# Five VectorE instructions per decoded weight tile in place of seven, with a second ScalarE pass and an integer addition

## The chip, the cores and the metric

The kernel runs on one core of one Trainium2 chip. The metric is the time of one execution on the device, in microseconds (us); lower is better. TensorE (PE) multiplies, VectorE (DVE) and ScalarE (ACT) do elementwise work, GpSimd (POOL) helps in the first stage, and SyncE (SP) issues the transfers.

## The reference

Three stages follow one another: a decayed linear attention over 2 x 8 heads of 768 positions and 64 features, a first dense block of two products with a gate between them, and a second dense block with a squared ReLU. The weights of both blocks are float64, because the scale factors make them so; all else is float32.

```python
for b in range(nb):                         # attention, 12 blocks of 64 positions
    intra = einsum(qb, kb) * Dmask @ vb
    inter = (qb * lam_pow) @ kv_state
    kv_state = lam_block * kv_state + (kb * rev_pow).T @ vb
x = out.transpose(0, 2, 1, 3).reshape(1536, 512)
h = x @ w_in                                # 512 x 2048
g = h * clip(h + 3, 0, 6) / 6
x = g @ w_out                               # 2048 x 512
h = maximum(x @ w_in2, 0)
return (h * h @ w_out2).astype(float32)
```

## The kernel before

**Attention** runs in 12 chunks of 128 positions. Per chunk PE makes scores (`scores`, line 315), DVE multiplies them with the decay (line 316), and PE makes the new state and the outputs (`state_values`, lines 331 to 356). ACT copies the outputs out rounded (`x_hi`, line 360) and DVE takes the remainder (`x_lo`, line 368).

**The two blocks** work on three blocks of 512 tokens. A product of float32 precision is three products of rounded halves: hi by hi, lo by hi, hi by lo. One *unit* is twelve matmuls of 512 columns. `hidden` is one unit for one tile `f` of 128 hidden features and one token block `j`; behind it ACT and DVE make `g`, its rounded half `gh` and its remainder `gl` (lines 407 to 415). `project` is one unit for 128 output features (first block) or 128 tokens (second block) over four tiles `f`; behind it DVE adds into `acc` (line 466), or ACT copies in the first group (line 463). There are 2 blocks x 4 groups x 3 token blocks x 8 units = 192 units. Between the four `hidden` units of one step stand the four `project` units of the step before: h(f0), four y, h(f1), h(f2), h(f3), then the next h(f0).

**Weights** arrive as float64 in 64 tiles of 128 x 512 (`raw`, two 32-bit words each). `decode_steps` (line 147) turns a tile into the pair `hi`, `lo`. ACT takes the magnitude of the high word's float view (`magnitude`, line 145), DVE clamps it (160), shifts it (164), joins sign and bits to the float `u` (170), ACT rounds `u` to `hi` (173), DVE isolates the exponent (177), scales the low word by it (181), takes `u - hi` (186) and adds (189). That is seven DVE steps and two ACT steps.

**Order.** All engines but SP run in the order in which the program writes instructions. A small planner decides where decode steps go: it counts 2.72 us for a unit, 0.44 or 0.7 us for a DVE step, 0.8 us for an ACT step (`UNIT, ONE, TWO, SCALAR`, line 28), and fills decode steps into DVE's queue up to the time at which the next result of PE is due (`decode_until`, `vector`, `unit`). In the attention it spends 1.15 us of decode per chunk from chunk 3 on (`ATT_FILL`). Decoded tiles live in 5 slots (7 after the attention) for `wi` and 7 for `wo`; a slot comes free behind the last token block that uses it. So three `wi` and three `wo` of the next group may be decoded ahead, and the fourth of each later.

Of the kernel before, what the change touches and what calls it, by code (L numbers as in the profile page):

```python
# [8 lines left out]
F32 = mybir.dt.float32  # L9
F32R = mybir.dt.float32r  # L10
BF16 = mybir.dt.bfloat16
I32 = mybir.dt.int32
U32 = mybir.dt.uint32
AF = mybir.ActivationFunctionType
ALU = mybir.AluOpType
PSUM = bass.MemoryType.PSUM

P = 128
# [9 lines left out]
UNIT, ONE, TWO, SCALAR = 2.72, 0.44, 0.7, 0.8  # L28
# [5 lines left out]
def decay_attention_moe_moe(  # L34
# [26 lines left out]
    nc = tc.nc  # L61
# [4 lines left out]
    NT, DM = out.shape  # L66
# [8 lines left out]
    dec = ctx.enter_context(tc.tile_pool(name="dec", bufs=2))  # L75
# [31 lines left out]
    keys = []  # L107
# [3 lines left out]
        for part in (fs[:n_ahead], fs[n_ahead:]) if i else (fs,):  # L111
            keys += [(kind, *x) for kind in ("wi", "wo") for x in part]
    n_loaded, n_begun = 0, 0
    raw_t, abs_t, w_t = {}, {}, {}
    w_free = {k: list(range(n)) for k, n in WBUFS.items()}
    w_slots = {}

    def w_tiles(kind):
        s = w_free[kind].pop(0)
        if (kind, s) not in w_slots:  # L120
            if s < WBUFS[kind]:
                pair = [wsp.tile([P, DM], F32R, name=f"{kind}{h}{s}") for h in ("h", "l")]
            else:
                pair = [ap.tile([P, DM], F32R, tag=("qs", "kd")[s - WBUFS[kind]], name=f"{kind}{h}{s}") for h in ("h", "l")]
            w_slots[kind, s] = pair
        return s, *w_slots[kind, s]
# [3 lines left out]
    def load_ahead(n):  # L130
        nonlocal n_loaded
        while n_loaded < min(n, len(keys)):
            kind, layer, f = keys[n_loaded]
            t = raw.tile([P, DM, 2], I32, tag="raw", name="raw")
            src = {"wi": (w_in1, w_in2), "wo": (w_out1, w_out2)}[kind][layer]
            nc.sync.dma_start(out=t.rearrange("p m w -> p (m w)"), in_=src[f])
            raw_t[n_loaded] = t
            n_loaded += 1

    def magnitude(n):  # L140

        if n < len(keys) and n not in abs_t:
            load_ahead(n + 1)
            abs_t[n] = dec.tile([P, DM], F32, tag="a", name="da")
            nc.scalar.activation(abs_t[n], raw_t[n][:, :, 1].bitcast(F32), AF.Abs, scale=2.0**16)  # L145

    def decode_steps(n):

        key = keys[n]
        kind = key[0]  # L150
        magnitude(n)
        t, a = raw_t.pop(n), abs_t.pop(n)
        lo32, hi32 = t[:, :, 0], t[:, :, 1]
        ai = a.bitcast(I32)
        u = dec.tile([P, DM], I32, tag="u", name="du")
        slot, hi, lo = w_tiles(kind)

        def clamp():

            nc.vector.tensor_scalar(a, a, 2.0, 1.875 * 2.0**32, op0=ALU.max, op1=ALU.min)  # L160
            magnitude(n + 1)

        def shift():
            nc.vector.tensor_scalar(
                ai, ai, 4, 1, op0=ALU.logical_shift_left, op1=ALU.logical_shift_right
            )

        def join():

            nc.vector.scalar_tensor_tensor(  # L170
                u, hi32, -(2**31), ai, op0=ALU.bitwise_and, op1=ALU.bitwise_or
            )
            nc.scalar.copy(hi, u.bitcast(F32))

        def power():

            nc.vector.tensor_scalar(ai, u, -(2**23), None, op0=ALU.bitwise_and)

        def lower():

            nc.vector.scalar_tensor_tensor(
                a, lo32.bitcast(U32), 2.0**-52, a, op0=ALU.mult, op1=ALU.mult
            )

        def rest():
            nc.vector.tensor_tensor(u.bitcast(F32), u.bitcast(F32), hi.bitcast(F32), op=ALU.subtract)

        def add():
            nc.vector.tensor_tensor(lo, u.bitcast(F32), a, op=ALU.add)  # L189
            w_t[key] = (hi, lo, slot)  # L190
            load_ahead(n + 1 + RAW)

        return [(ONE, clamp), (ONE, shift), (TWO, join), (ONE, power), (TWO, lower), (TWO, rest), (TWO, add)]

    def decode_piece():
        nonlocal n_begun
        if not pieces:
            if n_begun == len(keys):
                return 0
            if not w_free[keys[n_begun][0]]:  # L200
                return 0
            pieces.extend(decode_steps(n_begun))
            n_begun += 1
        cost, step = pieces.pop(0)
        step()
        return cost
# [382 lines left out]
```

## Time and profile before

| | |
|---|---|
| median of 3 executions | 579.88 us (579.8 to 581.48) |
| span of the profiled execution | 1483.6 us; no other time of it is recorded |
| busy in it: PE, DVE, ACT, POOL | 1477.0, 426.5, 256.6, 31.4 us |
| first matmul of the scores / of the first unit | 5.86 us / 107.5 us |
| DVE instructions | 723, of which 7 x 64 decode weights |

The profiled execution is two and a half times as long as the timed ones. Its PE rows can't be those of a timed execution, since 2304 matmuls of the units at the 595 ns from start to start that it shows come to 1371 us. DVE, ACT and POOL rows have no such conflict with the time. So PE's waits in a timed execution can't be read from this trace and have to be worked out from what the other engines must finish by when. A row of the timeline gives start and duration; the distance between two starts on one engine is what an instruction costs in a row of work, and may be less than its duration.

### The profile page before, as it was taken

The numbers are of one execution on the slowest core, as the hardware profiler recorded it, in microseconds if no ns is written. First come the engines' busy times: TensorE is split into PE (matmuls) and PEld (weight loads), VectorE is DVE, ScalarE is ACT, GpSimd is POOL, SyncE is SP. The second block draws the span as 40 slices with busy tenths as digits, with TensorE's granted clock in tenths as the row PEclk, the third lists the DMA queues.
The fourth block names the chain that finished last, engine by engine and source line by source line (L and its number), as shares of the span: only waits on it lengthen the run. The fifth ranks groups of instructions, "written<-read, shape, count | busy, mean of one in ns | idle before, by whom it ended". The sixth has DMA issues, their size and how long they took to land.

```text
span 1483.6 us, 7734 instructions
## 1 busy us (share of the span) xinstructions
PE 1477.0 (100%) x3022; PEld 885.7 (60%) x3022; DVE 426.5 (29%) x723; ACT 256.6 (17%) x417; POOL 31.4 (2%) x36
## 2 busy tenths in 40 slices
PE   9999999999999999999999999999999999999998
PEld 6775555555555555655555555555555555555555
DVE  3443333333323333133333331123312233010100
ACT  0112212111111121021121221121210221110100
POOL 2310000000000000000000000000000000000000
DMA  7400010101000100000000100000000000000000
GB/s 266 146 29 28 29 42 29 44 30 40 29 14 15 41 30 28 0 28 28 29 14 29 57 29 14 15 28 29 28 15 14 29 28 0 0 0 21 8 28 28
DMA packets 18035, 49.77 MB, mean 34 GB/s; under 512 B 2128, under 2 KB 2128, under 8 KB 18000
## 3 DMA queue, kind: packets, MB, share of 16 engines
q1 hardware_dynamic: 17856, 49.04, 9.7%
q8 instruction: 23, 0.38, 0.1%
q10 hardware_dynamic: 144, 0.26, 0.1%
q14 instruction: 12, 0.10, 0.0%
HBM read 46.14 MB, written 3.15 MB: 33 GB/s over the span
## 4 chain that ended last, share of the span: by engine, by line
PE 100%; DVE 0%; issue 0%
PE py L428 46%; PE ph L396 46%; PE psc L315 2%; PE pxt L356 2%; PE pxt L331 2%; PE pst L337 1%; PE warm L500 1%; DVE A L316 0%; DVE acc L466 0%; DVE idle L485 0%
## 5 line engine op out<-in xcount | busy, mean ns | idle before, releaser
L396 PE MATMUL ph<-xh,wil 128*128 128x512 f32 x384 | 318.1, 828 | 0.0
L396 PE MATMUL ph<-xl,wih 128*128 128x512 f32 x384 | 318.0, 828 | 0.0
L396 PE MATMUL ph<-xh,wih 128*128 128x512 f32 x384 | 318.0, 828 | 0.0
L396 PEld LDWEIGHTS ph<-xl,wih 128*128 128x128 f32 x384 | 135.3, 352 | 93.4 <-issue 93.4
L396 PEld LDWEIGHTS ph<-xh,wih 128*128 128x128 f32 x384 | 135.0, 352 | 93.7 <-issue 93.7
L396 PEld LDWEIGHTS ph<-xh,wil 128*128 128x128 f32 x384 | 135.2, 352 | 93.2 <-issue 93.1
L466 DVE TENSOR_TENSOR acc<-acc,py 128x512 f32<-128x512 f32 x72 | 49.6, 688 | 369.6 <-PE py L428 369.6
L409 DVE SCALAR_TENSOR_TENSOR g<-g,ph 128x512 f32<-128x512 f32 x48 | 33.0, 688 | 232.1 <-ACT g L407 232.1
L411 ACT ACTIVATE g<-ph 128x512 f32<-128x512 f32 x48 | 28.7, 598 | 323.7 <-PE ph L396 323.7
L428 PE MATMUL py<-gl,woh 128*128 128x512 f32 x96 | 79.7, 830 | 0.0
L428 PE MATMUL py<-gh,wol 128*128 128x512 f32 x96 | 79.5, 828 | 0.0
L428 PE MATMUL py<-gh,woh 128*128 128x512 f32 x96 | 79.5, 828 | 0.0
L428 PE MATMUL py<-woh,gh 128*128 128x512 f32 x96 | 79.4, 827 | 0.0
L428 PE MATMUL py<-woh,gl 128*128 128x512 f32 x96 | 79.3, 826 | 0.0
L428 PE MATMUL py<-wol,gh 128*128 128x512 f32 x96 | 79.3, 826 | 0.0
L415 DVE TENSOR_TENSOR gl<-g,gh 128x512 fp32r<-128x512 f32 x48 | 33.1, 689 | 151.4 <-ACT gh L413 151.4
L407 ACT ACTIVATE g<-ph,three 128x512 f32<-128x512 f32 x48 | 33.0, 688 | 234.8 <-PE ph L396 234.8
L145 ACT ACTIVATE da<-raw 128x512 f32<-128x512 f32 x64 | 42.7, 668 | 109.6 <-DVE wil L189 61.0
L428 PE MATMUL py<-woh,gA 128*128 128x512 f32 x64 | 52.7, 823 | 0.0
L428 PEld LDWEIGHTS py<-gh,wol 128*128 128x128 f32 x96 | 33.8, 352 | 23.5 <-issue 23.5
L428 PEld LDWEIGHTS py<-gh,woh 128*128 128x128 f32 x96 | 34.1, 355 | 23.1 <-issue 21.1
L428 PEld LDWEIGHTS py<-wol,gh 128*128 128x128 f32 x96 | 33.7, 351 | 23.5 <-issue 23.5
(94 smaller groups left out, 1430.5 us busy)
## 6 DMA issues: line engine op xcount, KB each, us to landing
raw<-in_w_in SPq DMA_DIRECT2D x32, 512.0 KB, 3.2
raw<-in_w_out SPq DMA_DIRECT2D x32, 512.0 KB, 3.2
out<-acc SPq DMA_DIRECT2D x12, 256.0 KB, 2.0
kT<-in_kT SPq DMA_DIRECT2D x6, 256.0 KB, 4.7
k<-in_k SPq DMA_DIRECT2D x6, 256.0 KB, 5.0
v<-in_v SPq DMA_DIRECT2D x6, 256.0 KB, 4.2
lent<-in_kT SPq DMA_DIRECT2D x6, 256.0 KB, 5.0
lent<-in_qT SPq DMA_DIRECT2D x6, 256.0 KB, 5.2
```

What stands on the lines that cost most here:

```text
L145: nc.scalar.activation(abs_t[n], raw_t[n][:, :, 1].bitcast(F32), AF.Abs, scale=2.0**16)
L315: nc.tensor.matmul(ps[:, t, a, :], kT_t[c][r, i], q_t[c][r, i], start=True, stop=True)
L331: nc.tensor.matmul(px[r, a, :], kv_old[r, a, :], qs_t[c][r, a, :], start=a == 0, stop=False, skip_group_check=True)
L337: nc.tensor.matmul(ps[halves[h % 2], h // 2, :], kd_t[c][:, h, :], v_t[c][:, h * D : (h + 1) * D], start=True, stop=True)
L356: nc.tensor.matmul(px[r, a, :], v_t[c][:, h * D : (h + 1) * D], A_t[c][:, a, t, :], start=first and a == 0, stop=True, skip_group_check=True,)
L396: nc.tensor.matmul(ph, w[:, a * P : (a + 1) * P], x[:, a, :], start=a == 0 and i == 0, stop=a == KD - 1 and i == 2,)
L407: nc.scalar.activation(g, ph, AF.Relu, bias=three)
L409: nc.vector.scalar_tensor_tensor(g, g, 6.0, ph, op0=ALU.min, op1=ALU.mult)
L411: nc.scalar.activation(g, ph, AF.Relu)
L415: nc.vector.tensor_tensor(gl, g, gh.bitcast(F32), op=ALU.subtract)
L428: nc.tensor.matmul(py, a, b, start=f == fs[0] and i == 0, stop=f == fs[-1] and i == 2)
L466: nc.vector.tensor_tensor(t, t, py, op=ALU.add)
```

## The change

The way to the low part changes. ACT now also converts the low word to an integer, scaled so that it stands in units of the last place of `u` (`up`, tile `dt`). DVE shifts the magnitude by 3 without the second shift, joins it as before, adds `up` to `u` as 32-bit integers, and takes `lo` as that sum minus `hi`. The exponent step and the scaling of the low word are gone. The clamp of tile n+1 now stands inside the steps of tile n, and the first tile's clamp stands ahead of all steps. The planner's constants stay; its list of costs per tile has five entries in place of seven.

```diff
         abs_t[n] = dec.tile([P, DM], F32, tag="a", name="da")
         nc.scalar.activation(abs_t[n], raw_t[n][:, :, 1].bitcast(F32), AF.Abs, scale=2.0**16)
+        up_t[n] = dec.tile([P, DM], I32, tag="t", name="dt")
+        nc.scalar.activation(up_t[n], raw_t[n][:, :, 0].bitcast(U32), AF.Copy, scale=2.0**-29)
+
+def clamp(n):
+    if n < len(keys):
+        nc.vector.tensor_scalar(abs_t[n], abs_t[n], 2.0, (1.875 - 2.0**-23) * 2.0**32, op0=ALU.max, op1=ALU.min)
...
-    def clamp():
-        nc.vector.tensor_scalar(a, a, 2.0, 1.875 * 2.0**32, op0=ALU.max, op1=ALU.min)
+    def shift():
+        nc.vector.tensor_scalar(ai, ai, 3, None, op0=ALU.logical_shift_left)
         magnitude(n + 1)
-    def shift():
-        nc.vector.tensor_scalar(ai, ai, 4, 1, op0=ALU.logical_shift_left, op1=ALU.logical_shift_right)
...
-    def power():
-        nc.vector.tensor_scalar(ai, u, -(2**23), None, op0=ALU.bitwise_and)
-    def lower():
-        nc.vector.scalar_tensor_tensor(a, lo32.bitcast(U32), 2.0**-52, a, op0=ALU.mult, op1=ALU.mult)
+    def add():
+        nc.vector.tensor_tensor(up, u, up, op=ALU.add)
     def rest():
-        nc.vector.tensor_tensor(u.bitcast(F32), u.bitcast(F32), hi.bitcast(F32), op=ALU.subtract)
-    def add():
-        nc.vector.tensor_tensor(lo, u.bitcast(F32), a, op=ALU.add)
+        nc.vector.tensor_tensor(lo, up.bitcast(F32), hi.bitcast(F32), op=ALU.subtract)
...
-    return [(ONE, clamp), (ONE, shift), (TWO, join), (ONE, power), (TWO, lower), (TWO, rest), (TWO, add)]
+    return [(ONE, shift), (TWO, join), (ONE, lambda: clamp(n + 1)), (TWO, add), (TWO, rest)]
```

The lines below the steps move up by six (`L409` is `L403`), and the steps stand on new lines: clamp 152, shift 167, join 172, rounding of `hi` 175, add 179, rest 182; the new ACT pass is line 147. PE's order is the same. DVE at the end of the attention and the start of the first units, before, from the last two steps of the third `wi` tile on:

```order
L186 TENSOR_TENSOR du<-du,wih_738 128x512
L189 TENSOR_TENSOR wil_739<-du,da 128x512
L160 TENSOR_SCALAR da<-da 128x512
L164 TENSOR_SCALAR da<-da 128x512
L170 SCALAR_TENSOR_TENSOR du<-raw,da 128x512
L409 SCALAR_TENSOR_TENSOR g<-g,ph 128x512
L177 TENSOR_SCALAR da<-du 128x512
L181 SCALAR_TENSOR_TENSOR da<-raw,da 128x512
L415 TENSOR_TENSOR gl_793<-g,gh_792 128x512
```

After, at the same place:

```order
L179 ISA dt<-du,dt 128x1024
L182 TENSOR_TENSOR wil_757<-dt,wih_756 128x512
L167 TENSOR_SCALAR da<-da 128x512
L172 SCALAR_TENSOR_TENSOR du<-raw,da 128x512
L152 TENSOR_SCALAR da<-da 128x512
L403 SCALAR_TENSOR_TENSOR g<-g,ph 128x512
L179 ISA dt<-du,dt 128x1024
L182 TENSOR_TENSOR wol_805<-dt,woh_804 128x512
L409 TENSOR_TENSOR gl_814<-g,gh_813 128x512
```

The decode is one tile further: where the third `wi` ended, the fourth ends now, and the first `wo` is complete before the first `gl`. The integer addition is an instruction of its own kind over 1024 half words (`ISA`, 128x1024).

ACT in one of the busiest stretches of `hidden` units of the second block (ReLU, square, rounding to `gh`, then decode work), before:

```order
L411 ACTIVATE g<-ph 128x512
L412 ACTIVATE g<-g 128x512
L413 CAST gv<-g 128x512
L145 ACTIVATE da<-raw 128x512
L173 CAST wih_1125<-du 128x512
L411 ACTIVATE g<-ph 128x512
L412 ACTIVATE g<-g 128x512
L413 CAST gh_816<-g 128x512
L145 ACTIVATE da<-raw 128x512
L173 CAST wih_1170<-du 128x512
```

After, in a stretch of the same kind:

```order
L405 ACTIVATE g<-ph 128x512
L406 ACTIVATE g<-g 128x512
L407 CAST gv<-g 128x512
L145 ACTIVATE da<-raw 128x512
L147 ACTIVATE dt<-raw 128x512
L175 CAST wih_1084<-du 128x512
L405 ACTIVATE g<-ph 128x512
L406 ACTIVATE g<-g 128x512
L407 CAST gh_838<-g 128x512
L145 ACTIVATE da<-raw 128x512
L147 ACTIVATE dt<-raw 128x512
L175 CAST woh_955<-du 128x512
```

Each decoded tile now puts three ACT instructions between two units' work, not two.

## Rows read from the trace of the kernel before

**Rows 1.** The page's part 1: busy us (share), instructions, of each engine.

```profile
PE 1477.0 (100%) x3022; PEld 885.7 (60%) x3022; DVE 426.5 (29%) x723; ACT 256.6 (17%) x417; POOL 31.4 (2%) x36
```

**Rows 2.** Chain that ended last, in time order: start, us, what.

```profile
343.50 28.58 PE ph L396 x48
```

**Rows 3.** Windows, attention and units: length, busy per engine, granted clock, DMA share, GB/s.

```profile
0.00:108.00 108.00, 105.48 (x719) 75.43 (x720) 42.04 (x65) 12.08 (x20) 31.39 (x36) 1.00 0.43 151
108.00:1484.00 1376.00, 1371.56 (x2304) 810.29 (x2302) 384.45 (x658) 244.49 (x398) 0.00 (x0) 1.00 0.07 24
```

**Rows 4.** Timeline: start, us; first scores on PE, last addition on DVE.

```profile
5.86 2.62 PE L315 MATMUL psc<-q,kT 64*128 64x128 f32 x16
1479.59 0.69 DVE L466 TENSOR_TENSOR acc<-acc,py 128x512 f32<-128x512 f32 x1 [6.49 <-PE py L428]
```

**Rows 5.** Groups by line, the two steps taken out: busy us, mean ns, idle before.

```profile
L181 DVE SCALAR_TENSOR_TENSOR da<-raw,da 128x512 f32<-128x512 uint32 x64 | 44.6, 696 | 2.0
L177 DVE TENSOR_SCALAR da<-du 128x512 int32<-128x512 int32 x64 | 27.4, 428 | 1.1
```

**Rows 6.** Timeline of DVE, one tile decoded without a wait, to the next.

```profile
199.38 0.42 DVE L160 TENSOR_SCALAR da<-da 128x512 f32<-128x512 f32 x1
199.83 0.43 DVE L164 TENSOR_SCALAR da<-da 128x512 int32<-128x512 int32 x1
200.29 0.69 DVE L170 SCALAR_TENSOR_TENSOR du<-raw,da 128x512 int32<-128x512 int32 x1
201.02 0.43 DVE L177 TENSOR_SCALAR da<-du 128x512 int32<-128x512 int32 x1
201.48 0.69 DVE L181 SCALAR_TENSOR_TENSOR da<-raw,da 128x512 f32<-128x512 uint32 x1
202.09 0.69 DVE L186 TENSOR_TENSOR du<-du,wih 128x512 f32<-128x512 f32 x1
202.81 0.69 DVE L189 TENSOR_TENSOR wil<-du,da 128x512 fp32r<-128x512 f32 x1
203.42 0.42 DVE L160 TENSOR_SCALAR da<-da 128x512 f32<-128x512 f32 x1
```

**Rows 7.** Timeline of DVE in the first units of block one.

```profile
115.56 0.69 DVE L409 SCALAR_TENSOR_TENSOR g<-g,ph 128x512 f32<-128x512 f32 x1 [3.84 <-ACT g L407]
...
117.23 0.68 DVE L415 TENSOR_TENSOR gl<-g,gh 128x512 fp32r<-128x512 f32 x1
117.83 0.68 DVE L186 TENSOR_TENSOR du<-du,wih 128x512 f32<-128x512 f32 x1
...
123.89 0.42 DVE L160 TENSOR_SCALAR da<-da 128x512 f32<-128x512 f32 x1
124.22 0.68 DVE L415 TENSOR_TENSOR gl<-g,gh 128x512 fp32r<-128x512 f32 x1
```

**Rows 8.** Groups by line, DVE's work per chunk of the attention.

```profile
L316 DVE TENSOR_TENSOR A<-psc,decay 128x1024 f32<-128x1024 f32 x12 | 14.7, 1224 | 17.9 <-PE psc L315 17.9
L367 DVE TENSOR_TENSOR xl<-pxt,xh 128x512 fp32r<-128x512 f32 x12 | 8.3, 690 | 18.0 <-ACT xh L360 18.0
L347 DVE TENSOR_TENSOR kv<-pst,kvs 128x256 f32<-128x256 f32 x8 | 3.4, 425 | 20.3 <-PE pst L337 17.6 <-POOL qs L297 2.6
```

**Rows 9.** Timeline of ACT behind one unit of block two.

```profile
865.11 0.60 ACT L411 ACTIVATE g<-ph 128x512 f32<-128x512 f32 x1 [6.07 <-PE ph L396]
865.74 0.63 ACT L412 ACTIVATE g<-g 128x512 f32<-128x512 f32 x1
866.40 0.62 ACT L413 CAST gh<-g 128x512 fp32r<-128x512 f32 x1
866.93 0.66 ACT L145 ACTIVATE da<-raw 128x512 f32<-128x512 f32 x1
867.49 0.60 ACT L173 CAST woh<-du 128x512 fp32r<-128x512 f32 x1
```

## What the change should do to the time, and why

> **What bounds the kernel now.** I read the page's busy table first [rows 1]: in the recorded execution PE is busy for 1477.0 of 1483.6 us, DVE for 426.5. That PE is saturated there proves little, since it ran far too slowly: a run of 48 matmuls of the units takes 28.58 us [rows 2], 595 ns each, and 2304 of them would fill 1371 us [rows 3] where a whole timed execution takes 579.88 us. The windows give a granted clock of 1.00, the 2.4 GHz level [rows 3], so the clock column doesn't explain it, and no other row does. I therefore make the sum against the timed median, 579.88 us, and take from the trace only the durations of DVE and ACT. DVE's 426.5 us are 74% of 579.88, ACT's 256.6 are 44%: DVE is loaded enough that PE could wait for it somewhere, and the question is where.
>
> What a unit of twelve matmuls takes in a timed execution no row shows. The kernel's own planner counts 2.72 us (line 28). 192 units are then 522.2 us. With 5.9 us ahead of the first scores and 4.0 us from the last addition's start to the end of the span [rows 4], the attention is left 579.88 - 522.2 - 9.9 = 47.8 us, 4.0 us for each of 12 chunks. If nothing but the start were outside the units, a unit would be (579.88 - 5.9)/192 = 2.99 us; if a column took one cycle at 2.4 GHz, it would be 12 x 512/2.4 = 2.56 us, an estimate. I take 2.72 and keep 2.56 as the hard case, because a faster PE asks for weights earlier.
>
> Now DVE's side. The stretch without a wait [rows 6] gives the cost of one tile from start to start: 203.42 - 199.38 = 4.04 us. `g` and `gl` cost 0.61 each in a full queue (117.23 to 117.83, [rows 7]), an `acc` the same by its like shape. Two places could make PE wait:
>
> 1. *The first units.* When the first unit begins, DVE owes the last two steps of the third `wi` (0.72 + 0.61 = 1.33), the fourth `wi` and four `wo` (5 x 4.04 = 20.2), and behind twelve `hidden` units 24 instructions for `g` and `gl` (24 x 0.61 = 14.6): 36.1 us. The last `wo` is wanted by unit 15 (counted from 0), after 15 x 2.72 = 40.8 us, or 38.4 at 2.56. Spare: 4.7 or 2.3 us.
> 2. *The later groups of the first block.* A group of 24 units asks of DVE 8 tiles and 36 instructions: 32.3 + 22.0 = 54.3 us, of 65.3 us at 2.72 or 61.4 at 2.56. The tile with least room is the fourth `wo`, whose slot comes free five units before it is wanted: 12.8 us at 2.56, for 4.0 us of decode and four units' `g` and `gl`, 4.9 us. The second block has no `g` on DVE and asks less.
>
> So by these sums DVE is heavily used but in time, and the units are bound by PE. That is the base of the forecast.
>
> **The change part by part.** *Taken out:* the exponent step and the scaling of the low word, 428 and 696 ns [rows 5]. *Exchanged:* a float addition for an integer one. By the distances of [rows 6] a tile now costs: shift to join 0.46; join to the next clamp, which doesn't need it, 0.61 (as 201.48 to 202.09); clamp to addition 0.34 (as 123.89 to 124.22, [rows 7]); addition to rest, which needs it, 0.72 (as 202.09 to 202.81); rest to the next shift 0.61. The sum is 2.74 us, 1.30 less, or 83 us of DVE time over 64 tiles.
>
> The addition itself is not in the trace. Its nearest rows are the joins and sums over 128x512, 690 to 696 ns [rows 5, 8], and from above the product over 128x1024 elements, 1224 ns [rows 8], since the instruction names 1024 half words. No DVE row with two inputs of 512 or more elements is below 680, so I see no gain below that. I take the lower, because the bytes are those of 512 words; with the upper a tile costs 3.27 us, still 0.77 less than before.
>
> The Trainium skill ("VectorE: DVE Perf Modes", section "Mode 2×_1P — pack two bf16 into one 32-bit read") says that a two-input instruction on packed 16-bit elements handles two of them in a cycle. By that rule 1024 half words cost what 512 words do, and the tile is at 2.74 us; without it, at 3.27. No row of before can show it.
>
> *Added on ACT:* one pass per tile. In a full queue its sister, the magnitude, costs 0.56 us (866.93 to 867.49) and alone 0.66 [rows 9]: 36 to 42 us over 64 tiles, ACT going from 257 to about 295 us of 580. Its cover: in the first block, per group of 24 units, ACT has 12 ReLU and 12 roundings and 8 tiles, some 31 us of 61 or more after the change. Without that cover it would delay the ReLU behind it by 0.56 us.
>
> *Attention.* The planner still spends 1.15 us per chunk. Before, that paid for two tiles and five steps of a third: 8.08 + 2.6 = 10.7 us. Now it pays for three tiles, three more steps and the first clamp, which the planner doesn't count: 8.22 + 1.41 + 0.45 = 10.1 us, or 11.7 with the dear addition (3 x 0.53 more). DVE's other work per chunk is 1.22 + 0.69 + 0.43 = 2.3 us at most [rows 8], with decode 3.5 of the chunk's 4.0 us, so most of a difference of -0.6 to +1.0 us is hidden behind PE. I count half of the gain, -0.3 us. One transfer of 512 KB moves ahead of two chunks' inputs on SP; it waits for a `raw` slot that is free by then, and the chunk behind it is wanted four chunks later. I count nothing; if the transfers were late, it would cost what half a chunk's 1 MB takes.
>
> *First units.* The decode comes in one tile further: DVE owes 1.33 + 4 x 2.74 + 14.6 = 26.9 us instead of 36.1. PE wasn't waiting there, so the 9.2 us are idle time. *Later groups:* 54.3 becomes 43.9 us; again idle time. *End:* no tile is decoded in the last group's stretch, nothing changes.
>
> The sum: 579.88 - 0.3 = **579.6 us**. What a measurement of this kernel can tell from no change is about 0.3%, 1.7 us, so this forecast is "no difference".
>
> **The rivals.**
>
> *Faster: DVE was late in the first units.* My sum lets DVE work without a gap. But from `g` to `gl` it takes 1.67 us (115.56 to 117.23 [rows 7]) with two decode steps between them, because `gl` needs ACT's rounding. If only those two steps fit into each of the twelve units, 24 of the 37 steps are done when the twelfth `g` is due, and 13 remain, at 0.58 us (4.04/7) 7.5 us. The last `wo` is ready at 12 units + 0.8 + 2.3 + 7.5, 41.3 us at 2.56 and 43.2 at 2.72, that is 2.9 or 2.4 us late. After the change 22 steps are left where 24 fit, and the wait is gone: 577.0 us. If each of the four groups of the first block held such a wait, four times 2.9 is 11.6 us and the time 568.3. For it speaks DVE's 83 to 88% in the first block; against it that the rows of the order put more than two steps into some units, and that the later groups have 7 us of room or more. Chance 0.26, mostly for one or two such waits.
>
> The Trainium skill ("TensorE: Matmul & The Clock Gate", section "Wait — 56ns, not 53.3ns?") gives 215.7 ns from start to start for warm matmuls of 512 columns. By that a unit takes 2.59 us, the attention would be left 73 us, and PE would be nearer to the hard case of this rival. The recorded 595 ns can't decide it.
>
> *Slower: ACT takes DVE's place.* In the second block ACT has ReLU, square and rounding behind each `hidden`, 1.82 us (865.11 to 866.93 [rows 9]), and in the dense stretches a tile's three passes more, 3 x 0.56 = 1.7 us: 3.5 us in a unit of 2.72 (2.56). Two such units in a row leave ACT 1.6 (2.0) us late. The project units need `gl` of the last `hidden` 1.9 units after its end, 5.2 (4.9) us; the way there is the lag, 1.8 us on ACT and 0.7 on DVE, 4.1 (4.5) us without what the queues add. So it decides once queues add 1.1 (0.4) us, for example DVE held at the next tile's clamp, which now waits for an ACT pass issued only one step earlier. There are three such stretches; if each costs PE the whole lag, 4.8 to 6 us: 585 us. Against it: ACT catches up in the four project units that follow, and a stall would have to use up all the spare. Chance 0.14.
>
> *The change doesn't do what it says:* the addition costs 1224 ns or more. Only from 2.0 us on would a tile cost DVE more than before. With 1224 the attention adds 1.0 us at most, 580.9, within what can't be told from no change. Chance 0.08.
>
> **How the numbers follow.** The forecast has 0.52, the dear addition 0.08: no difference 0.60. Faster 0.26, slower 0.14. The time is that of the forecast, 579.6 us. For 8 in 10 the range takes the forecast, the dear addition, the rival of late weights as far as two and a half waits (2.5 x 2.9 = 7.2 us, down to 572.6) and the ACT rival as far as two of its three stretches at the lower price (2 x 1.6 = 3.2, up to 583.1). That leaves out about 0.07 below and 0.07 above.
>
> **What would show it right or wrong.** In the profile after: five decode lines of 64 instructions on DVE; the addition at about 0.69 us, not 1.22; DVE's busy time down by some 72 us (64 x (0.428 + 0.696)) to 355; ACT's up by about 42 to 299; in a stretch without a wait 2.74 us from one tile's shift to the next. PE's order is the same, so if the recording again slows PE, its span should not move at all, and only the timed executions can speak. The forecast is wrong if they differ from 579.88 by more than 1.7 us. A gain would say that PE did wait for decoded weights, and the spare of 2.3 to 4.7 us in the first units is the step that fails; a loss would point to ACT's queue, or to DVE held at the clamp.

## The result, and the profile after

| | before | after |
|---|---|---|
| median of the executions | 580.65 us (579.8 to 581.48, 4 of them) | 584.5 us (584.16 to 584.93, 4 of them) |
| ratio after to before, 95% interval | | 1.0068 [1.0049, 1.0086] |
| span of the profiled execution | 1483.6 us | 582.4 us |

The changed kernel is 0.7% slower, some 3.9 us by the medians. That is more than the 0.3% that a measurement of this kernel can tell, and it lies above the predicted range (572.6 to 583.1 us).

This time the recording has PE at the speed of a timed execution. Page of after, part 1 (busy us, share, instructions), where before had [rows 1]:

```profile
PE 570.5 (98%) x3022; PEld 470.0 (81%) x3022; DVE 349.4 (60%) x595; ACT 287.2 (49%) x481; POOL 31.5 (5%) x36
```

The edit did to the engines what it says. Groups of the page of after (busy us, mean ns | idle before): the integer addition and the added ACT pass.

```profile
L179 DVE CUSTOM_DVE_ANT_0 dt<-du,dt 128x1024 uint16<-128x1024 uint16 x64 | 44.3, 692 | 0.0
L147 ACT ACTIVATE dt<-raw 128x512 int32<-128x512 uint32 x64 | 42.7, 668 | 15.8 <-DVE wil L182 8.5
```

The addition takes 692 ns, as the lower bound had it. In the dense stretch of DVE a tile now goes from shift to shift in 95.24 - 92.44 = 2.80 us, against 4.04 in [rows 6]. Timeline of DVE in after (start, us, what):

```profile
92.44 0.42 DVE L167 TENSOR_SCALAR da<-da 128x512 int32<-128x512 int32 x1
...
95.24 0.42 DVE L167 TENSOR_SCALAR da<-da 128x512 int32<-128x512 int32 x1
```

So the question is where PE lost time although DVE has less to do. The waits of PE in after (line, for whom: us in total, times, longest) name two places in the kernel's own work (a third entry of 1.2 us, left out here and below, is in the warm-up matmuls at the start):

```profile
PE psc L309 <- DVE A L310: 3.9, 3, 2.3
PE py L422 <- ACT acc L457: 2.5, 1, 2.5
...
```

The chain of work that ended last in after (start, us, what) comes back to PE behind the same two waits, at 27.53 and at 101.35 us. From 53 us on, in between, it runs over DVE, ACT and one weight transfer, not over PE, which still has work then. [Rows 2] had 28.58 us for 48 matmuls, where now 10.88 stand:

```profile
27.53 1.40 PE psc L309 x16
28.93 1.90 PE pxt L325 x16
...
61.78 0.68 ACT dt L147
...
62.97 0.59 ACT g L401
63.59 0.69 DVE g L403
...
99.84 1.47 ACT acc L457 x3
101.35 8.47 PE py L422 x36
...
112.54 10.88 PE py L422 x48
```

From 101.4 us on the chain is PE's own work, after the first 36 matmuls at 10.88 us per 48, 2.72 per unit, and PE waits for nobody. What the change costs is paid ahead of that: at 27.5 us, in the attention, and at 101.4 us, behind the first sums of the first block.

### The profile page after: what moved, and what is told of

It is laid out like the page before. It is cut to its first block, busy times and chain, and to the rows that moved or that the text cites. A ratio compares the mean times of both kernels' runs of the same rounds, so it can differ in the third digit from the quotient of the medians.

```text
span 582.4 us, 7659 instructions
## 1 busy us (share of the span) xinstructions
PE 570.5 (98%) x3022; PEld 470.0 (81%) x3022; DVE 349.4 (60%) x595; ACT 287.2 (49%) x481; POOL 31.5 (5%) x36
## 4 chain that ended last, share of the span: by engine, by line
PE 89%; DVE 5%; ACT 3%; issue 1%; DMA 1%; POOL 0%; SPq 0%; DVEq 0%; ACTq 0%; POOLq 0%
PE py L422 43%; PE ph L390 39%; PE psc L309 2%; PE pxt L325 2%; PE pxt L350 2%; DVE g L403 1%; PE pst L331 1%; ACT g L401 1%; DMA k<-in_k 1%; DVE dt L179 1%; DMA raw<-in_w_out 1%; DVE du L172 0%; ACT dt L147 0%; DVE A L310 0%; DVE da L152 0%
## 5 line engine op out<-in xcount | busy, mean ns | idle before, releaser
L390 PE MATMUL ph<-xh,wih 128*128 128x512 f32 x384 | 149.5, 389 | 0.0
L390 PE MATMUL ph<-xh,wil 128*128 128x512 f32 x384 | 149.4, 389 | 0.0
L390 PE MATMUL ph<-xl,wih 128*128 128x512 f32 x384 | 149.4, 389 | 0.0
L390 PEld LDWEIGHTS ph<-xh,wih 128*128 128x128 f32 x384 | 72.1, 188 | 15.1 <-ACT dt L147 0.2
L390 PEld LDWEIGHTS ph<-xl,wih 128*128 128x128 f32 x384 | 72.1, 188 | 14.9
L390 PEld LDWEIGHTS ph<-xh,wil 128*128 128x128 f32 x384 | 72.1, 188 | 14.9
L409 DVE TENSOR_TENSOR gl<-g,gh 128x512 fp32r<-128x512 f32 x48 | 33.1, 689 | 54.1 <-ACT gh L407 54.0
L403 DVE SCALAR_TENSOR_TENSOR g<-g,ph 128x512 f32<-128x512 f32 x48 | 32.9, 686 | 35.2 <-ACT g L401 35.2
L147 ACT ACTIVATE dt<-raw 128x512 int32<-128x512 uint32 x64 | 42.7, 668 | 15.8 <-DVE wil L182 8.5
L172 DVE SCALAR_TENSOR_TENSOR du<-raw,da 128x512 int32<-128x512 int32 x64 | 44.8, 700 | 1.7
L401 ACT ACTIVATE g<-ph,three 128x512 f32<-128x512 f32 x48 | 32.9, 685 | 26.2 <-PE ph L390 26.2
L179 DVE CUSTOM_DVE_ANT_0 dt<-du,dt 128x1024 uint16<-128x1024 uint16 x64 | 44.3, 692 | 0.0
L422 PE MATMUL py<-gh,wol 128*128 128x512 f32 x96 | 37.4, 389 | 0.0
```

Source lines behind the costliest of these rows:

```text
L147: nc.scalar.activation(up_t[n], raw_t[n][:, :, 0].bitcast(U32), AF.Copy, scale=2.0**-29)
L172: nc.vector.scalar_tensor_tensor(u, t[:, :, 1], -(2**31), ai, op0=ALU.bitwise_and, op1=ALU.bitwise_or)
L179: nc.vector.tensor_tensor(up, u, up, op=ALU.add)
L390: nc.tensor.matmul(ph, w[:, a * P : (a + 1) * P], x[:, a, :], start=a == 0 and i == 0, stop=a == KD - 1 and i == 2,)
L401: nc.scalar.activation(g, ph, AF.Relu, bias=three)
L403: nc.vector.scalar_tensor_tensor(g, g, 6.0, ph, op0=ALU.min, op1=ALU.mult)
```

## The experiments

**What the kernel before really does.** The first recording of before couldn't show PE's waits, so it was recorded again, unchanged.

> The kernel before, unchanged, profiled once more, because its first trace shows PE at 595 ns per matmul and hides where PE waits. The kernel after shows two waits of PE: 2.25 us for VectorE's product with the decay of chunk 5 in the attention, behind which the granted clock falls to 0.57 of full for some 4 us, and 2.53 us at 98.8 us for ScalarE's copies of the first projected sums. Theory 'two waits': both are absent or much shorter here, and PE takes 2.72 us per unit throughout. Rival 'the passes themselves cost PE time': the waits are here too, and the 3.9 us lie spread over the units, which then take less than 2.72 us here.

Measured: 579.74 us, span 577.9, 48 matmuls of the units in 10.88 us. Waits of PE, the kernel before recorded again (same columns), and its PE timeline at the attention's wait:

```profile
PE psc L315 <- DVE A L316: 3.7, 3, 2.0
...
```

```profile
27.50 1.16 PE L315 MATMUL psc<-q,kT 64*128 64x128 f32 x16 [1.99 <-DVE A L316]
```

Two things follow. The unit of 2.72 us was right, and no unit of before waits for weights, so the rival "faster" had nothing to gain. But PE does wait before the change too, 2.0 us in the attention for DVE's product with the decay. So of the two waits of after one is old (1.99, now 2.25 us) and one is new: the 2.5 us for ACT's copies. All runs below are about that second wait, the first wait, and what makes them.

**The copies queue behind the decode.** The first group's sums are copied out of PSUM by ACT (line 457, four copies). In after they stand in ACT's queue behind the passes of three tiles. Timeline of ACT in after, and PE's first matmul behind the wait:

```profile
94.15 0.67 ACT L145 ACTIVATE da<-raw 128x512 f32<-128x512 f32 x1
95.36 0.68 ACT L147 ACTIVATE dt<-raw 128x512 int32<-128x512 uint32 x1 [0.54 <-DVE wil L182]
96.42 0.62 ACT L175 CAST woh<-du 128x512 fp32r<-128x512 f32 x1 [0.39 <-DVE du L172]
...
99.22 0.62 ACT L175 CAST woh<-du 128x512 fp32r<-128x512 f32 x1 [0.39 <-DVE du L172]
99.75 2.04 ACT L457 COPY acc<-py 128x512 f32<-128x512 f32 x4
```

```profile
101.35 0.50 PE L422 MATMUL py<-gh,woh 128*128 128x512 f32 x1 [2.53 <-ACT acc L457]
```

PE had the four sums ready at 95.8 us (units from 52.27 us on, 16 x 2.72 = 43.5). ACT starts to copy them at 99.75, since it has to do each tile's rounding first, and that waits for DVE's join. A unit later PE needs a PSUM buffer that the copies have not yet freed. The edit puts the copies ahead of the decode steps of that unit; nothing else changes:

```diff
             products(layer, j, grp, e, f, py_t[e])
-        unit()
         if f == GROUP * (grp + 1) - 1:
             for e in range(KD):
                 project(layer, j, grp, e, py_t.pop(e))
+        unit()
```

> The kernel after, with ScalarE's four copies of the first projected sums written ahead of the last unit's decode steps instead of behind them, so that one tile's three passes less stand in front of them. Theory 'two waits': the 2.53 us wait of PE at 98.8 us goes, 584.5 - 2.5 = 582.0 us, a ratio to before of 1.002. Rival 'the attention alone': no change, 584.5. Rival 'the passes cost PE time everywhere': no change, 584.5.

Measured over 11 executions: 581.49 us, ratio to before 1.0009 [1.0001, 1.0018]. The copies come one tile earlier (counted from the units' start, 44.7 us in place of 47.5), and the wait is gone. ACT and the waits of PE in this kernel:

```profile
96.09 2.05 ACT L457 COPY acc<-py 128x512 f32<-128x512 f32 x4
```

```profile
PE psc L309 <- DVE A L310: 3.9, 3, 2.3
...
```

The place of the copies is worth 3.0 us by the medians (584.5 to 581.49), or 3.4 by the ratios (0.0059 of 580.65): nearly the whole loss. Six of these executions have about the mean clock of after, 0.995 or 0.996, and a median of 581.5 us, so the 3.0 us are not the clock's. The run shows which wait cost the time, not yet why ACT came there so late.

**Which part makes ACT late: the pass or the pace?** Two things changed for ACT: a third pass per tile, and a planner that believes a tile to cost 2.98 us of DVE (0.44, 0.7, 0.44, 0.7, 0.7) and not 4.12, and so packs steps closer. Three kernels separate them. *The old pace with the new steps*, the five costs raised to a sum of 4.12:

```diff
-        return [(ONE, shift), (TWO, join), (ONE, lambda: clamp(n + 1)), (TWO, add), (TWO, rest)]
+        return [(0.60, shift), (0.97, join), (0.61, lambda: clamp(n + 1)), (0.97, add), (0.97, rest)]
```

> The kernel after, with the planner told that a tile's five steps cost 4.12 us in sum as the seven did (0.60, 0.97, 0.61, 0.97, 0.97), so that decode steps stand about as far apart in the queues as before; the instructions are those of the kernel after. Theory 'it is where the steps are put': one tile instead of three stands in front of the copies, the wait at 98.8 us goes and the time is 581 to 582 us (1.001 to 1.002). Rival 'the third ScalarE pass or the integer addition costs PE time by itself': 584.5 us (1.007), since all of them are still there.

*The new pace without the pass:* the low word's bits aren't added. A tile of zeros, set up once at the start (not shown below), is added instead, and all else is as in after.

```diff
             up_t[n] = dec.tile([P, DM], I32, tag="t", name="dt")
-            nc.scalar.activation(up_t[n], raw_t[n][:, :, 0].bitcast(U32), AF.Copy, scale=2.0**-29)
...
-            nc.vector.tensor_tensor(up, u, up, op=ALU.add)
+            nc.vector.tensor_tensor(up, u, none, op=ALU.add)
```

> The kernel after without ScalarE's third pass per tile: the integer addition adds a tile of zeros instead of the converted low word, so the low part lacks the low word's bits; all else, the order of VectorE included, is that of the kernel after. Theory 'three passes at the denser pace': ScalarE starts the ReLU of the first twelve units up to 4.07 us after the unit's end in the kernel after and 1.35 in the kernel before; without the pass the lateness falls below 2 us, VectorE keeps to the plan, the copies stand in front of PE in time, and the time is about 582 us (ratio 1.002). Rival 'density alone', three tiles in front of the copies whatever they cost: the wait of 2.5 us and 584.5 us (1.006) stay.

*The old steps and pace with the pass:* before, with an ACT pass more per tile whose result nobody reads.

```diff
             nc.scalar.activation(abs_t[n], raw_t[n][:, :, 1].bitcast(F32), AF.Abs, scale=2.0**16)
+            spare = dec.tile([P, DM], I32, tag="t", name="dt")
+            nc.scalar.activation(spare, raw_t[n][:, :, 0].bitcast(U32), AF.Copy, scale=2.0**-29)
```

> The kernel before with ScalarE's extra pass over the low word added per tile (its result is not used), seven VectorE steps and their pace as before. Theory 'three passes at the denser pace': at the old pace ScalarE has room, at most 0.5 us of change, 580.9 to 581.4 (1.000 to 1.001). Rival 'the pass costs time wherever it stands': about 3 us more, 584 (1.005).

How late ACT is, I read from its timeline: start of the ReLU (line 401 or 407) less the end of its unit (units' start plus 2.72 for each), for the first twelve units.

| kernel | pace | pass | ratio to before | ReLU late, most (twelfth) | copies, after the units' start |
|---|---|---|---|---|---|
| before, recorded again | old | no | | 1.35 (0.41) | 42.6 |
| before_third_pass | old | yes | 1.0011 [1.0002, 1.0019] | 2.71 (1.49) | 42.7 |
| old_pace | old | yes | 0.9997 [0.9987, 1.0008] | 1.64 (0.88) | 42.5 |
| no_third_pass | new | no | 1.0013 [1.0004, 1.0022] | 2.22 (1.31) | 44.7 |
| after | new | yes | 1.0068 [1.0049, 1.0086] | 4.07 (4.07) | 47.5 |

Only the last has a wait for the copies. The medians of the three came out somewhat below what the first theory expected: 580.7 us with the unread pass (580.9 to 581.4 expected), 580.34 at the old pace (581 to 582) and 580.79 without the pass (about 582). ACT's timeline at the copies, in the kernel without the pass and then in the one with the old pace:

```profile
95.94 0.62 ACT L174 CAST woh<-du 128x512 fp32r<-128x512 f32 x1 [1.61 <-DVE du L171]
96.47 2.04 ACT L456 COPY acc<-py 128x512 f32<-128x512 f32 x4
```

```profile
94.58 2.06 ACT L457 COPY acc<-py 128x512 f32<-128x512 f32 x4 [4.64 <-PE py L422]
```

At the old pace ACT waits for PE there, 4.64 us; without the pass it starts to copy 1.2 us behind the end of the sums, which PE doesn't notice; with both it is 4.0 us behind. Neither part alone costs more than 0.13% by the medians (0.22% at the upper ends of the intervals). It takes the third pass *and* the closer packing. What the pass does in the first units shows in ACT's own timeline in after: the rounding of the first unit, the second unit, then one tile's three passes ahead of the third ReLU.

```profile
58.15 0.62 ACT L407 CAST gh<-g 128x512 fp32r<-128x512 f32 x1 [0.75 <-DVE g L403]
58.68 0.68 ACT L401 ACTIVATE g<-ph,three 128x512 f32<-128x512 f32 x1
60.68 0.62 ACT L407 CAST gh<-g 128x512 fp32r<-128x512 f32 x1 [1.32 <-DVE g L403]
61.21 0.69 ACT L145 ACTIVATE da<-raw 128x512 f32<-128x512 f32 x1
61.78 0.68 ACT L147 ACTIVATE dt<-raw 128x512 int32<-128x512 uint32 x1
62.34 0.63 ACT L175 CAST woh<-du 128x512 fp32r<-128x512 f32 x1
62.85 0.70 ACT L401 ACTIVATE g<-ph,three 128x512 f32<-128x512 f32 x1
```

ACT goes from the ReLU to the rounding of the same unit and waits in between for DVE's `g`. That costs it 1.32 us here and never less than 0.75, and the next instruction in its queue doesn't use the gap. The chain shown with the result runs through this same stretch: the tile's passes on ACT, the late ReLU behind them, then DVE's `g`. Windows and ACT's waits from the first unit to the twelfth ReLU in after sum it up (window: length, then busy per engine in the order PE, PEld, DVE, ACT, POOL):

```profile
52.27:88.98 36.71, 36.71 (x164) 30.39 (x163) 29.92 (x53) 24.59 (x42) 0.00 (x0) 1.00 0.27 87
```

```profile
ACT gh L407 <- DVE g L403: 6.0, 6, 1.5
ACT gv L407 <- DVE g L403: 1.7, 2, 0.9
ACT gkT L407 <- DVE g L403: 1.5, 2, 0.8
ACT gA L407 <- DVE g L403: 1.3, 1, 1.3
```

Busy 24.59 us and 10.5 us of waits for `g` make 35.1 of 36.71 us; the rest are waits ahead of the first ReLU. Busy time and waits fill any engine's time. What tells a full one is that it doesn't wait for the source of its work, and here no ReLU waits for PE: ACT is full in this stretch, although it is busy for only 67% of it. In before recorded again ACT is busy for 19.20 of 33.05 us up to the twelfth ReLU (58%), its waits for `g` are 9.1 us, and its ReLUs still wait for PE, 1.1 us in all. In before_third_pass and no_third_pass, which have one part each, no ReLU waits for PE over these units either, but the lateness stays at 2.71 us or less and falls back; with both parts it grows to 4.07. That the waits for `g` are what fills ACT is read from these rows; no run took them away. DVE, for its part, waits for the late ReLU. Its waits ahead of `g` over the first twelve units, in after and in before recorded again:

```profile
DVE g L403 <- ACT g L401: 5.5, 6, 1.3
```

```profile
DVE g L409 <- ACT g L407: 2.4, 4, 0.7
```

So the two engines that were to share the work pass their lateness to each other.

**The pace alone, on the old steps.** If packing steps closer than they run is what starts it, before must suffer from it as well. Here its seven steps cost the planner 2.98 us per tile instead of 4.12:

```diff
-        return [(ONE, clamp), (ONE, shift), (TWO, join), (ONE, power), (TWO, lower), (TWO, rest), (TWO, add)]
+        return [(0.32, clamp), (0.32, shift), (0.51, join), (0.31, power), (0.50, lower), (0.51, rest), (0.51, add)]
```

> The kernel before with the planner told that its seven steps cost 2.98 us in sum, the figure of the five: the old instructions at the new pace. Theory 'a queue filled faster than it is worked off makes the copies late': a tile takes VectorE 4.04 us and three stand in front of ScalarE's copies, so VectorE falls behind by about 1 us per tile in the first units and PE waits for the copies longer than in the kernel after: 585 to 590 us (1.007 to 1.016). Rival 'only the new instructions matter': 580.9 (1.000).

Measured: 619.62 us, ratio 1.0677 [1.0662, 1.0692]. The kind of loss is as expected, the size is not: 39.7 us, several times what I had put. Waits of PE in this kernel:

```profile
PE psc L315 <- DVE A L316: 8.9, 7, 2.0
PE py L428 <- ACT acc L463: 7.6, 1, 7.6
PE py L428 <- DVE gq L415: 5.4, 7, 1.2
...
```

Here the same wait for the copies is 7.6 us, the attention's waits are 8.9, and waits for `gl` come on top, because a tile really takes DVE 4.04 us [rows 6] and the planner counts 2.98. In after a tile takes 2.80 and the planner counts 2.98, so DVE itself fits; what the planner doesn't count is ACT. The listed waits don't add up to the 39.7 us. By the two profiles PE stands idle 26.2 us longer than in before recorded again (35.2 us of 618.1, against 9.0 of 577.9) and is busy 14.0 us longer for the same 3022 matmuls (582.9 against 568.9), at a mean granted clock of 0.985 in place of 1.000: a third of the loss is slower matmuls.

**The wait in the attention.** DVE's product with the decay for chunk 5 comes late, for the first decode steps stand ahead of it. DVE in after, there:

```profile
22.85 0.64 DVE L152 TENSOR_SCALAR da<-da 128x512 f32<-128x512 f32 x1 [1.58 <-ACT da L145]
...
25.33 0.42 DVE L152 TENSOR_SCALAR da<-da 128x512 f32<-128x512 f32 x1
25.66 0.69 DVE L361 TENSOR_TENSOR xl<-pxt,xh 128x512 fp32r<-128x512 f32 x1
26.26 1.22 DVE L310 TENSOR_TENSOR A<-psc,decay 128x1024 f32<-128x1024 f32 x1
```

The first clamp waits 1.58 us for ACT's magnitude (1.58 in before recorded again, too). The line of the next clamp, 0.33 us from start to start, is what the change adds here. If the 1.58 us are what matters, an earlier magnitude takes the wait away:

```diff
         state_values(c)
+        if c == 2:
+            magnitude(0)
```

> The kernel after, with ScalarE's two passes over the first tile written behind chunk 2 instead of chunk 3, so that VectorE's first clamp doesn't wait for them. Theory 'two waits': VectorE reaches the product of chunk 5 about 1.5 us earlier, PE's 2.25 us wait there shrinks to 0.7 or less, the clock stays at full, 584.5 - 1.5 - 1.6 = 581.4 us (ratio 1.001). Rival 'the opening units alone': 584.5.

Measured: 583.93 us, ratio 1.0056 [1.0043, 1.0070], where 581.4 was expected: a miss. The wait for the magnitude is gone, but PE's wait at chunk 5 falls only from 2.25 to 1.83 us. The clock stays at full there (1.00 from 26 to 34 us), and the units start at 50.31 us, 1.96 us earlier than in after. Most of that is lost again further on: behind the 2.54 us wait for the copies the clock falls in this recording (0.83 over 100 to 110 us, where after has 1.00). The chain here has 10.07 us for the 36 matmuls that take 8.47 in after:

```profile
99.40 10.07 PE py L422 x36
```

So the attention did get shorter, and 1.6 us went to the clock at the other wait. That PE's wait shrank so little is the other part of the miss. DVE in this kernel:

```profile
21.63 0.73 DVE L167 TENSOR_SCALAR da<-da 128x512 int32<-128x512 int32 x1
22.39 1.65 DVE L172 SCALAR_TENSOR_TENSOR du<-raw,da 128x512 int32<-128x512 int32 x1
23.97 1.28 DVE L152 TENSOR_SCALAR da<-da 128x512 f32<-128x512 f32 x1
```

The steps start 1.7 us earlier than in after and then take 0.73, 1.65 and 1.28 us in place of the 0.42, 0.69 and 0.42 of the dense stretch. POOL is multiplying over this time (22.04 to 24.96 us without a gap). The Trainium skill ("Trainium Architecture — The Big Picture", section "What this means for kernel authors") says that of the engines only DVE and GpSimd contend for a shared pair of SBUF ports, with an exclusive lock. The rows agree as far as they go: the long steps lie beside POOL's work, those of the dense stretch have POOL idle. No run here moved POOL's work away, so the cause isn't shown.

**Moving the decode out of that stretch.** The last kernel is an attempt at a better version: after, with decode from chunk 7 on in place of 3, the magnitude one chunk ahead, and a tile counted at 3.53 us.

```diff
-        return [(ONE, shift), (TWO, join), (ONE, lambda: clamp(n + 1)), (TWO, add), (TWO, rest)]
+        return [(0.52, shift), (0.83, join), (0.52, lambda: clamp(n + 1)), (0.83, add), (0.83, rest)]
...
-        if c >= 3:
+        if c == 6:
+            magnitude(0)
+        if c >= 7:
             owed += ATT_FILL
```

> The kernel after with three changes of order: decode in the attention starts behind chunk 7 instead of 3, ScalarE's passes over the first tile behind chunk 6, and the planner counts 3.53 us per tile, between the two paces. Theory: the wait of PE at chunk 5 (2.0 us before, 2.25 after) goes, since VectorE has no decode there, and the copies are in time: 580.3 - 2.0 = 578.3 us (0.996). Rival 'the wait only moves to the chunk behind the first decode steps': 580.3 (0.999).

Measured over 11 executions: 579.2 us, ratio 0.9983 [0.9974, 0.9992], against 578.3 expected. It is the fastest kernel here, below before by 0.17%, which the interval separates from no change but which is little. At chunk 5 the 2 us wait for DVE is gone, and half of it is a wait for a transfer now. The rival was right in part too: behind the first decode steps, which now stand later, PE waits 0.64 us for DVE. PE at both places in this kernel:

```profile
26.39 1.16 PE L309 MATMUL psc<-q,kT 64*128 64x128 f32 x16 [1.14 <-DMA q<-in_qT]
...
41.65 1.16 PE L309 MATMUL psc<-q,kT 64*128 64x128 f32 x16 [0.64 <-DVE A L310]
```

The DMA engines are busy around chunk 5 in after and in before recorded again: share 1.03 and more, some 400 GB/s, in the windows further below. So behind the wait for DVE stands one for a transfer, 1.14 us here. The recording shows no gain in the attention as a whole: from the second chunk's scores to the first unit it takes 41.69 us (8.74 to 50.43), against 41.55 in before recorded again (9.15 to 50.70). Part of the 0.17% is the clock, which stays at a mean of 0.998 or more in all 11 executions: the 21 of before's 27 with such a clock have a median of 579.86 us, 0.7 above the 579.2.

## Why the prediction was wrong

*Right.* The base in the dense blocks: a unit of 2.72 us, 192 of them, DVE in time. The terms on DVE: the addition at the lower price (692 ns against 690 to 696), the tile at 2.80 us against 2.74, DVE's busy time 349.4 against 355. ACT's 287.2 us are 12 below the 299 that I gave: from 255.2 in before recorded again they are 0.50 us for each of the 64 passes, nearer to the 0.56 of a full queue than to the 0.66 that I took. The Trainium skill's rule on packed 16-bit elements that stood beside the addition ("VectorE: DVE Perf Modes", section "Mode 2×_1P — pack two bf16 into one 32-bit read") agrees with the 692 ns. That there is no gain, since PE wasn't waiting for weights, holds as well: with the pace put back, the new steps give 0.9997 [0.9987, 1.0008], although DVE has 70 us less to do (420.0 in before recorded again, 349.4 in after).

*The step that failed: the cover of the added ACT pass, at the pace at which the tiles then came.* I counted ACT's work in the first block by busy time, "some 31 us of 61 or more", took the rest as free, and priced an uncovered pass at 0.56 us. The rest isn't free. ACT stands still between a unit's ReLU and its rounding until DVE has made `g`, 0.75 us at the least. With 0.95 us of such waits a unit and one tile's passes every two units the engine is full, and what comes on top adds up: the ReLU is 1.73 us late at the first unit and 4.07 at the twelfth. The trace of before had the rows for this. [Rows 7] show `gl` starting 1.67 us behind `g` because of the rounding between them, and I used them for DVE's queue but not for ACT's.

*The other half of it is the "idle time" of the first units.* The kernel before with the unread pass (1.0011) shows that at the old pace the pass was covered. I let DVE finish 9.2 us earlier, called that "idle time", and put its effect at nothing. It didn't stay idle. The planner filled the room with tiles that are wanted later (ACT rounds 6 tiles in the first twelve units, 4 in before), each with its three passes on ACT, and a part of it went ahead of `g`, where DVE waits for the ReLU (5.5 us, not 2.4). The spare that I checked, for the last weights, was not used up; no unit waits for weights. What ran out was a spare I hadn't listed: that of the four copies, which stand in ACT's queue behind decode work and free PE's sums. In before ACT starts them 0.9 us ahead of the last sum's end, as soon as PE has the first, in after 4.0 us behind it (42.6 and 47.5 us after the units' start, against 43.5).

*The rival "ACT takes DVE's place"* had the engine and the kind of mechanism right (three passes per tile where a unit's own work stands, lateness that queues add up), and the place wrong. I put it into the second block, where ACT has most busy time per unit. There it costs nothing: the waits of PE in after list no wait behind the first block's first sums. The busiest stretch was not the one with least room, and the second block has no exchange with DVE between ReLU and rounding [rows 9]; that this is why it had room is my reading. Its price, 585 us, was near the 584.5 measured, for a reason that was not its own. Its chance of 0.14 was too low by this: the pass was the one part of the change that took room, and I looked for its room in shares of busy time.

*The attention.* I counted -0.3 us and put the bounds at -0.6 and +1.0. PE waits 0.3 us longer at chunk 5 (2.25 against 1.99), and in the kernel with the copies moved, at full clock as before recorded again, the way from the second chunk's scores to the first unit takes 42.12 us (9.26 to 51.38) against 41.55 (9.15 to 50.70). That is 0.6 us, inside the bounds and of the other sign than the value that I took. (Two sums of the prediction are off by 0.1 us: the five steps of the third tile are 2.71 us by [rows 6], not 2.6, and the ACT rival's lag at 2.56 is 1.9, not 2.0. Nothing hangs on either.) I had not seen that PE waits there at all: the first recording has PE too slow for it.

*The account.* Of 4.47 us between the chain's ends of after and of before recorded again (578.27 and 573.80 us), 2.53 are the wait for the copies and 0.31 the slow start behind it (8.47 in place of 8.16 us for 36 matmuls); 1.57 are in the attention. There the second chunk's scores start 0.36 us earlier than in before (8.79 against 9.15 us), the way from them to the scores that wait at chunk 5 is 0.39 longer (18.74 against 18.35, 0.26 of it the wait), and the chunk behind takes 5.15 us in place of 3.60. In the kernel with the copies moved that chunk takes 3.69 at full clock, so 1.46 of it are the clock, told below, and some 0.5 to 0.6 in the attention belong to the change. The timed executions bear the split out: all of after have a mean clock of 0.996 or 0.997, and against the 581.24 us that is the median of before's executions at 0.996 the 584.5 are 3.3 us more, near 2.53 + 0.31 + 0.5. The other 0.6 of the 3.9 us go with the clock, which not all executions of before have as low. Open is why the chunks around chunk 5 are longer by some 0.1 us each, and whether the change makes the clock fall more often.

## What to carry to other kernels

An engine that takes turns with another one on the same data is full long before its busy share says so: count its waits inside the turn, 0.75 to 1.5 us here, with its work, before laying a new pass on it. When work goes from one engine to another, list everything that stands behind it in the second engine's queue and holds a buffer, not only what the moved work makes; here it was four copies out of PSUM, and putting them ahead of the decode gave back 3 us. And a planner that packs by one engine's costs can overfill another: this one counts a tile by its steps on DVE and nothing for its passes on ACT.

## What the runs showed of the hardware

**The clock can fall behind a wait of 2 us.** In after, PE's granted clock is 0.58 and 0.57 in the two windows behind the attention's wait, near its level of 1.2 GHz; in the 2 us before that PE had been busy for 0.47 us. Windows of after (granted clock, DMA share and GB/s are the last three):

```profile
26.00:28.00 2.00, 0.47 (x8) 0.47 (x10) 2.00 (x4) 0.55 (x2) 0.11 (x1) 1.00 1.03 401
28.00:30.00 2.00, 2.00 (x26) 1.78 (x24) 1.90 (x4) 0.00 (x0) 2.00 (x2) 0.58 1.06 407
30.00:32.00 2.00, 2.00 (x30) 1.67 (x29) 1.18 (x3) 0.00 (x0) 1.58 (x2) 0.57 1.06 398
```

and of before recorded again, where the wait is 0.3 us shorter and the clock stays:

```profile
26.00:28.00 2.00, 0.50 (x8) 0.50 (x10) 2.00 (x4) 0.85 (x2) 0.14 (x1) 1.00 1.03 400
28.00:30.00 2.00, 2.00 (x40) 1.71 (x40) 1.97 (x4) 0.00 (x0) 2.00 (x2) 1.00 1.05 405
```

By their chains the scores take 1.40 us and the first outputs 1.90 in place of 1.16 and 1.02, and from these scores to the next chunk's it takes 5.15 us, against 3.69 in the kernel with the copies moved, which has the same wait of 2.3 us at full clock: the fall costs some 1.5 us. So the length of the wait alone doesn't decide it: the recordings with the old pace and with the unread pass had a wait of 1.9 us and a clock of 0.54 and 0.50 from 28 to 30 us, behind it, and the recording with the early magnitude has the fall behind the wait for the copies. The same kernel falls in one execution and not in another; of 21 timed executions of before beside the first four experiments the 11 with a mean clock of 0.996 took 580.88 to 581.59 us, the 10 others 579.4 to 580.84. All four executions of after have 0.996 or 0.997. The kernel that starts to decode later stays at 0.998 or above in all 11.

**A matmul of 512 columns takes 227 ns here** (10.88 us for 48). The Trainium skill's 215.7 ns from start to start ("TensorE: Matmul & The Clock Gate", section "Wait — 56ns, not 53.3ns?") is 5% below that. The measurement decides: with it the prediction's doubt on the length of a unit would have been gone, and with it the hard case.

**The first recording of before was no picture of a timed execution.** Its 595 ns per matmul did not come back in any recording that followed, of the same kernel or another; the cause isn't known. Its DVE and ACT rows agree with the later ones (DVE 426.5 and 420.0 us, ACT 256.6 and 255.2), so the durations drawn from it held, and only what depends on PE's pace, above all who waits for whom, was missing.
